# Smaller first loads at the front and a reordered tail in a fused attention and gated-MLP kernel

## The chip, the core and the metric

The kernel runs on one core of a Trainium2 chip. The metric is the device time of one execution in microseconds (us). Engines: PE does matmuls, DVE and ACT do element-wise work, POOL is little used here, SP and ACT issue the DMA transfers. In this kernel PE writes its products into banks of a memory called PSUM (names beginning with ps_), from where DVE and ACT read them. The clock "granted" to PE is the share of full speed that its throttle let through. "PV" is the product of the attention weights and V. A "tile" is 128 rows of x.

## The reference

```python
xn = layernorm(x)                                   # x: 2048 x 512, bf16
s  = softmax((xn @ wq) K^T * 128**-0.5) V @ wo      # 32 heads of 128, 2048 cached keys
g  = silu( (relu(xn @ W_gate) * (xn @ W_up)) @ W_down )   # 512 -> 1792 -> 512
return x + s * g
```

## The kernel before

The program is: a head (layer norm of the first four tiles and the first three 128-column blocks of gate and up), the rest of the gated MLP, 32 heads of attention, and a tail (the output projection of the last heads, times g, plus x). Only head and tail concern us.

Loads of the front, in order of issue. `FCS` cuts the 14 weight blocks into load groups of 3, 5 and 6 blocks; a row of the first group is 3 x 128 x 2 = 768 bytes:

```python
FCS = [0, min(3, FC), min(8, FC), FC]
load_x0(sp, 0);  load_x0(act, 1)                 # one 128-row tile each
load_w(sp, Wg, 0);  load_w(act, Wu, 0)           # gate on SP's queue, up on ACT's
load_x0(sp, 2);  load_x0(act, 3)
load_w(sp, Wg, 1);  load_w(sp, Wu, 1);  load_xq(1)   # ... and the rest, all on SP
```

The head's PE order (`warm_mm` are dummy matmuls that raise the PE clock; `head_transpose` ends in a copy on ACT):

```python
_wait(pe, warm_w);  warm_mm(10)                  # operand cleared by DVE
ctok = {0: head_transpose(0, head_center(0))}
warm_mm(2)
for n in range(4):
    if n + 1 < 4: ntok = head_center(n + 1)      # statistics and centering on DVE
    _wait(pe, ctok[n])
    head_tile(n, 0)                              # gate and up of tile n, block 0
    if n + 1 < 4: ctok[n + 1] = head_transpose(n + 1, ntok)
    for fc in range(1, 3): head_tile(n, fc)
# then blocks 3..13, 512 rows at a time, through a ring of three PSUM bank pairs
```

The tail, for each of the last eight tiles (PE projects, DVE multiplies by g and adds to x, SP stores):

```python
mtok = dve.tensor_tensor(fin_tmp[fb], ps_r[bank], g_sb[n], mult)
_wait(dve, mtok)
ftok = dve.tensor_tensor(x_sb[n], x_sb[n], fin_tmp[fb], add)   # then SP stores x_sb[n]
...
for n in range(NT - 8, NT - 4, 2): emit_M([final n, final n + 1])
flush_last_transposes()              # PE transposes and ACT copies for the last four tiles
for n in range(NT - 4, NT, 2):     emit_M([final n, final n + 1])
```

The softmax here doesn't subtract the row's maximum and nothing guards it: scores larger than these inputs give would overflow.

Of the kernel before, what the change touches and what calls it, by code (L numbers as in the profile page):

```python
# [5 lines left out]
BF16 = mybir.dt.bfloat16  # L6
F32 = mybir.dt.float32
ALU = mybir.AluOpType
ACTF = mybir.ActivationFunctionType
# [42 lines left out]
def bass_recurrent_scan__mha_block_cached__glu_gated_reglu__prompt_kernel(  # L52
# [12 lines left out]
    _, S, D = A_x.shape  # L65
# [39 lines left out]
    with ExitStack() as es:  # L105
        _cnt = [0]

        def S_(shape, dt, name):
            _cnt[0] += 1
            return es.enter_context(nc.sbuf_tensor(f"{name}_{_cnt[0]}", shape, dt))  # L110
# [4 lines left out]
        def newsem(unit=1):  # L115
            _cnt[0] += 1
            return _Sem(es.enter_context(nc.semaphore(f"sem{_cnt[0]}")), unit)
# [13 lines left out]
        Wq_sb = [S_([128, DC, Dh], BF16, "Wq_sb") for _ in range(2)]  # L131
        Wo_sb = [S_([128, G, D], BF16, "Wo_sb") for _ in range(2)]
        PT = [S_([128, 2, NQ], BF16, "PT") for _ in range(NPB)]
        warm = S_([128, D], BF16, "warm")
        es_b = ExitStack()

        def SB_(shape, dt, name):
# [19 lines left out]

        sem_x = [newsem(16) for _ in range(QB)]
        sem_x0 = [newsem(16) for _ in range(4)]
        sem_wg = [newsem(16) for _ in range(3)]  # L160
        sem_wu = [newsem(16) for _ in range(3)]
        sem_xq = [newsem(16) for _ in range(QB)]
        sem_wd = newsem(16)
        sem_kt = [newsem(16), newsem(16)]
# [37 lines left out]
        with nc.Block() as block:  # L202

            @block.tensor
            def _(_pe_eng):
# [10 lines left out]
                for b in range(2):  # L216
                    tok_pool = sem_pool.sig(pool.memset(V_sb[b][:, :, Dh:VW], 2.0))

                FCS = [0, min(3, FC), min(8, FC), FC]
                HFC = 3  # L220
                wg_src = B_W_gate.rearrange("(c p) f -> p c f", p=128)
                wu_src = B_W_up.rearrange("(c p) f -> p c f", p=128)
# [1 line left out]
                def load_w(eng, dst, src, sems, k):  # L224
                    a, b_ = FCS[k] * 128, FCS[k + 1] * 128
                    if b_ > a:
                        sems[k].sig(eng.dma_start(dst[:, :, a:b_], src[:, :, a:b_]))
# [1 line left out]
                x0_tok = {}  # L229
                x_tok = {}  # L230

                def load_x0(eng, n):
                    x0_tok[n] = sem_x0[n].sig(eng.dma_start(x_sb[:, n:n + 1, :], x_t[:, n:n + 1, :]))

                def load_xq(Q):
                    x_tok[Q] = sem_x[Q].sig(
                        sp.dma_start(x_sb[:, 4 * Q:4 * Q + 4, :], x_t[:, 4 * Q:4 * Q + 4, :]))

                warm_w = sem_ln1.sig(dve.memset(warm[:], 0.0))
                load_x0(sp, 0)  # L240
                load_x0(act, 1)
                load_w(sp, Wg_sb, wg_src, sem_wg, 0)
                load_w(act, Wu_sb, wu_src, sem_wu, 0)
                load_x0(sp, 2)
                load_x0(act, 3)
                load_w(sp, Wg_sb, wg_src, sem_wg, 1)
                load_w(sp, Wu_sb, wu_src, sem_wu, 1)
                if QB > 1:
                    load_xq(1)
                load_w(sp, Wg_sb, wg_src, sem_wg, 2)  # L250
                load_w(sp, Wu_sb, wu_src, sem_wu, 2)
                for Q in range(2, QB):
                    load_xq(Q)
                sem_wd.sig(sp.dma_start(Wd_sb[:], B_W_down.rearrange("(c p) d -> p c d", p=128)))
# [101 lines left out]
                def head_transpose(n, ntok):  # L356
# [12 lines left out]
                    acc_free[n % 2] = sem_xa.sig(act.copy(xcT[:, :, n * 128:(n + 1) * 128], src))  # L369
                    return acc_free[n % 2]  # L370

                def warm_mm(k):
                    for _i in range(k):
                        pe.matmul(ps_r[:, 2 * NSLOT - 1, 0:D], warm[:, 0:128], warm[:], start=True, stop=True)

                def head_ln():
                    ctok = {0: head_transpose(0, head_center(0))}
                    warm_mm(2)
                    for n in range(4):
                        if n + 1 < 4:  # L380
                            ntok = head_center(n + 1)
                        _wait(pe, ctok[n])
                        head_tile(n, 0)
                        if n + 1 < 4:
                            ctok[n + 1] = head_transpose(n + 1, ntok)
                        for fc in range(1, HFC):
                            head_tile(n, fc)

                half_slots = []

                def head_tile(n, fc):
                    hs = slice(n * 128, (n + 1) * 128)
                    fs = slice(fc * 128, (fc + 1) * 128)
                    if n == 0:
                        half_slots.append(ring_acquire())
                    s = half_slots[fc]
                    for i, (W, sems) in enumerate(((Wg_sb, sem_wg), (Wu_sb, sem_wu))):
                        if n == 0 and fc == 0:
                            pe.wait_ge(sems[0].h, 16)
                        ins = None  # L400
                        for c in range(DC):
                            ins = pe.matmul(ps_r[:, 2 * s + i, hs], W[:, c, fs], xcT[:, c, hs],  # L402
                                            start=(c == 0), stop=(c == DC - 1))
                        if n == 3:
                            half_tok[(fc, i)] = (sem_gate if i == 0 else sem_gu).sig(ins)
# [39 lines left out]
                sig_free = [None, None]  # L445
                hT_free = [None, None]

                def finish_gate_up(Q, fc, s, gtok, gu_tok):
                    par = Q % 2
                    gb = 2 * s  # L450
                    gk = fc % NSLOT
                    _wait(act, gtok)
                    _wait(act, gr_free[gk])
                    rtok = sem_relu.sig(act.activation(gr_sb[gk][:], ps_r[:, gb, :], ACTF.Relu))  # L454
                    _wait(dve, gu_tok)
                    _wait(dve, rtok)
                    if fc == 0:
                        _wait(dve, hT_free[par])
                    h_tok = sem_h.sig(
                        dve.tensor_tensor(hT[par][:, fc, :], gr_sb[gk][:], ps_r[:, gb + 1, :], ALU.mult)  # L460
                    )
                    gr_free[gk] = h_tok
                    ring_tok[s] = [rtok, h_tok]
                    if Q == 0:
                        ln_task(fc)
                    return h_tok

                def emit_gate_up(Q):
                    qs = slice(Q * NQ, (Q + 1) * NQ)
                    h_tok = None  # L470
                    for fc in range(FC):
                        fs = slice(fc * 128, (fc + 1) * 128)
                        if Q == 0 and fc < HFC:
                            s = half_slots[fc]
                            finish_gate_up(Q, fc, s, half_tok[(fc, 0)], half_tok[(fc, 1)])
                            continue
                        s = ring_acquire()
                        gb = 2 * s
                        if fc == 0:
                            _wait_all(pe, xt_ready[Q])  # L480
                        xT, xs = (xcT, slice(0, NQ)) if Q == 0 else (xnT, qs)
                        if Q == 0 and fc in FCS:
                            k = FCS.index(fc)
                            pe.wait_ge(sem_wg[k].h, 16)
                            pe.wait_ge(sem_wu[k].h, 16)
                        ins = None
                        for c in range(DC):
                            ins = pe.matmul(ps_r[:, gb, :], Wg_sb[:, c, fs], xT[:, c, xs],  # L488
                                            start=(c == 0), stop=(c == DC - 1))
                        gtok = sem_gate.sig(ins)  # L490
                        for c in range(DC):
                            ins = pe.matmul(ps_r[:, gb + 1, :], Wu_sb[:, c, fs], xT[:, c, xs],  # L492
                                            start=(c == 0), stop=(c == DC - 1))
                        gu_tok = sem_gu.sig(ins)
                        h_tok = finish_gate_up(Q, fc, s, gtok, gu_tok)
                    return h_tok
# [39 lines left out]
                    hT_free[par] = ytok  # L536

                assert DC == 4 and QB >= 2 and FC >= 4 * (QB - 1) + 2
                _wait(pe, warm_w)
                warm_mm(10)  # L540
                head_ln()
                for Q in range(QB):
                    hlast = emit_gate_up(Q)
# [5 lines left out]
                rz_sb = S_([128, 4, 1], F32, "rz_sb")  # L549
                Onorm = [S_([128, 4, Dh], BF16, "Onorm") for _ in range(NON)]  # L550
                OT_store = [S_([128, G, S], BF16, "OT_store") for _ in range(2)]
                fin_tmp = [S_([128, D], BF16, "fin_tmp") for _ in range(2)]

                qt_ready = {}
                qp_done_tok = {}
# [213 lines left out]
                def emit_final_tile(n, bank):  # L769
# [8 lines left out]
                    for hh in range(G):  # L778
# [6 lines left out]
                    _wait(dve, fin_free[fb])  # L785
                    mtok = sem_opa.sig(
                        dve.tensor_tensor(fin_tmp[fb][:], ps_r[:, bank, 0:D], g_sb[:, n, :], ALU.mult))  # L787
                    _wait(dve, mtok)
                    if n == 0:
                        _wait(dve, base_done[NT - 1])  # L790
# [3 lines left out]
                    if Q == QB - 1 or j % 2 == 1:  # L794
                        n0 = n if Q == QB - 1 else n - 1
                        _wait(sp, ftok)
                        sem_out.sig(sp.dma_start(out_t[:, n0:n + 1, :], x_sb[:, n0:n + 1, :]))
                    return mtok

                plan = {}  # L800
                for b in range(NBLK):
# [47 lines left out]
                assert not plan  # L849
                for n in range(NT - 8, NT - 4, 2):  # L850
                    emit_M([(emit_final_tile, n), (emit_final_tile, n + 1)])
                flush_last_transposes()
                for n in range(NT - 4, NT, 2):
                    emit_M([(emit_final_tile, n), (emit_final_tile, n + 1)])
                sp.wait_ge(sem_out.h, sem_out.n)


# [26 lines left out]
```

## Time and profile before

| | before |
|---|---|
| median of the first 3 runs | 1287.48 us (1286.75 to 1287.56) |
| span of the profiled execution | 1286.0 us |
| first 512-wide gate matmul | 13.63 us |
| first gate matmul of the second 512 rows | 44.70 us |
| from the start of the last 32 PV matmuls (shown at 1272.37) to the end | 13.58 us |

The page rounds spans to 0.1 us. Stretches up to the end of the span are worked out here with the unrounded spans of the packed traces: 1285.957 us before, 1288.623 us after the change.

The page's busy table and its chain that ended last, of the kernel before:

```profile
PE 1279.3 (99%) x12040; PEld 835.4 (65%) x12040; DVE 382.0 (30%) x685; ACT 1001.7 (78%) x1109; POOL 13.2 (1%) x25
PE 98%; DVE 1%; DMA 0%; issue 0%; ACT 0%; ACTq 0%
```

PE bounds the kernel. What a change at the ends can win is PE's idle time there. The waits of PE, kernel before (engine, tile, line, who was waited for, total us, times, longest us):

```profile
PE ps_r L374 <- DVE warm L239: 1.2, 1, 1.2
PE ps_r L402 <- DMA Wu_sb<-in_B_W_up_dram: 0.5, 1, 0.5
PE ps_r L779 <- ACT OT_store L719: 0.4, 1, 0.4
PE ps_r L488 <- ACT gr_sb L454: 0.4, 1, 0.4
PE ps_r L402 <- ACT xcT L369: 0.2, 1, 0.2
```

Five waits, all at the two ends. The PE timeline of the front, kernel before (start us, length us, engine, line, operation, out<-in, shapes, count, and in brackets the idle time before it and who ended it):

```profile
1.19 4.23 PE L374 MATMUL ps_r<-warm 128*128 128x512 bf16 x10 [1.19 <-DVE warm L239]
5.26 0.39 PE L364 MATMUL ps_acc<-ident,xc_sb 128*128 128x128 bf16 x4
...
6.33 0.40 PE L402 MATMUL ps_r<-xcT,Wg_sb 128*128 128x128 bf16 x4 [0.25 <-ACT xcT L369]
7.23 0.40 PE L402 MATMUL ps_r<-xcT,Wu_sb 128*128 128x128 bf16 x4 [0.51 <-DMA Wu_sb<-in_B_W_up_dram]
...
13.63 1.02 PE L488 MATMUL ps_r<-xcT,Wg_sb 128*128 128x512 bf16 x4 [0.41 <-ACT gr_sb L454]
```

Ten warm-up matmuls take 0.42 us each, which is half rate; later ones of the same size start every 0.22 us. The first tile must wait for the up weights until 7.23, and the first 512-wide matmul waits for a PSUM bank pair until 13.63.

In the tail DVE is the limit. The end of its timeline, kernel before (multiply L787, add L792):

```profile
1281.72 0.68 DVE L787 TENSOR_TENSOR fin_tmp<-ps_r,g_sb 128x512 bf16<-128x512 f32 x1
1282.43 0.43 DVE L792 TENSOR_TENSOR x_sb<-x_sb,fin_tmp 128x512 bf16<-128x512 bf16 x1
1282.78 0.68 DVE L787 TENSOR_TENSOR fin_tmp<-ps_r,g_sb 128x512 bf16<-128x512 f32 x1
1283.49 0.42 DVE L792 TENSOR_TENSOR x_sb<-x_sb,fin_tmp 128x512 bf16<-128x512 bf16 x1
```

Read the differences of the starts: from a multiply to the add that depends on it 0.71, from that add to the next multiply 0.35, so 1.06 us a tile. Compare two independent DVE instructions of the same length, near 13 us of the same kernel, which start 0.60 us apart:

```profile
12.84 0.69 DVE L460 TENSOR_TENSOR hT<-gr_sb,ps_r 128x512 bf16<-128x512 bf16 x1 [3.27 <-PE ps_r L402]
13.44 0.69 DVE L319 BATCH_NORM_STATS2 stats<-x_sb 128x6 f32<-128x512 bf16 x1
```

### The profile page before, as it was taken

Reading aid. Unit: us, or ns where it says so; the run is one execution under the profiler, and the core shown is the slowest. Engines: PE = TensorE matmul, PEld = TensorE weight load, DVE = VectorE, ACT = ScalarE, POOL = GpSimd, SP = SyncE. Lnnn points to the kernel's source line nnn. Section 1 sums busy time; section 2 is a strip of 40 time slices with the busy share of each in tenths; the row PEclk is TensorE's granted clock in tenths of the full one; section 3 lists DMA queues with packets and bytes.
Section 4 is the critical chain, followed back from the end, with each engine's and each line's share of the span. In section 5 each row is a group of like instructions: output and inputs, shape, how many; then the busy total and the mean of one; then the engine's idle time right before and its main releaser. Section 6 shows DMA issues by size and latency. Waiting matters only on the chain.

```text
span 1286.0 us, 26948 instructions
## 1 busy us (share of the span) xinstructions
PE 1279.3 (99%) x12040; PEld 835.4 (65%) x12040; DVE 382.0 (30%) x685; ACT 1001.7 (78%) x1109; POOL 13.2 (1%) x25
## 2 busy tenths in 40 slices
PE   9999999999999999999999999999999999999998
PEld 5444466666666666666666666666666666666665
DVE  6433311112222222222222222222222222234456
ACT  3322399998888888888888888888888888888884
POOL 2100000000000000000000000000000000000000
PEclk9999999999999999999999999999999999999999
DMA  9600123332222332332221322323323212332302
GB/s 262 131 1 1 21 44 52 63 57 38 37 54 47 71 54 50 55 70 51 54 46 33 64 47 53 55 67 55 55 50 71 54 34 38 52 65 55 50 14 74
DMA packets 240977, 72.13 MB, mean 56 GB/s; under 512 B 227808, under 2 KB 240864, under 8 KB 240864
## 3 DMA queue, kind: packets, MB, share of 16 engines
q1 hardware_dynamic: 240048, 69.76, 28.4%
q8 instruction: 96, 1.57, 0.5%
q10 hardware_dynamic: 816, 0.66, 0.2%
q14 instruction: 17, 0.14, 0.0%
HBM read 32.77 MB, written 2.10 MB: 27 GB/s over the span
## 4 chain that ended last, share of the span: by engine, by line
PE 98%; DVE 1%; DMA 0%; issue 0%; ACT 0%; ACTq 0%
PE ps_acc L742 36%; PE ps_r L645 34%; PE ps_r L578 9%; PE ps_r L599 8%; PE ps_acc L511 4%; PE ps_r L488 4%; PE ps_r L492 4%; PE ps_r L779 1%; DMA Wu_sb<-in_B_W_up_dram 0%; DVE fin_tmp L787 0%; PE ps_r L402 0%; ACT gr_sb L454 0%; DVE x_sb L792 0%; PE ps_acc L364 0%; DVE Onorm L696 0%
## 5 line engine op out<-in xcount | busy, mean ns | idle before, releaser
L655 ACT ACTIVATE PT<-ps_r 128x1024 bf16<-128x1024 f32 x1024 | 952.5, 1054 | 167.7 <-PE ps_r L645 167.7
L742 PEld LDWEIGHTS ps_acc<-V_sb,PT 128*128 128x128 bf16 x8192 | 621.1, 98 | 241.7 <-ACT PT L655 3.5
L742 PE MATMUL ps_acc<-V_sb,PT 128*128 128x129 bf16 x8192 | 776.7, 220 | 0.0
L645 PE MATMUL ps_r<-QT_sb,KT_sb 128*128 128x512 bf16 x2048 | 754.2, 379 | 0.0
L672 DVE RECIPROCAL rz_sb<-ps_acc 128x4 f32<-128x4 f32 x127 | 23.3, 184 | 729.5 <-PE ps_acc L742 729.5
L645 PEld LDWEIGHTS ps_r<-QT_sb,KT_sb 128*128 128x128 bf16 x2048 | 194.9, 98 | 1.1 <-DVE QT_sb L589 0.4
L578 PE MATMUL ps_r<-xnT,Wq_sb 128*128 128x512 bf16 x512 | 130.9, 379 | 0.0
L599 PE MATMUL ps_r<-Wo_sb,OT_store 128*128 128x512 bf16 x448 | 114.6, 379 | 0.0
L589 DVE CAST QT_sb<-ps_r 128x512 bf16<-128x512 f32 x128 | 88.5, 692 | 48.1 <-PE ps_r L578 48.1
L578 PEld LDWEIGHTS ps_r<-xnT,Wq_sb 128*128 128x128 bf16 x512 | 49.9, 97 | 60.6 <-ACT PT L655 27.1
L675 DVE TENSOR_TENSOR Onorm<-ps_acc,rz_sb 128x512 bf16<-128x512 f32 x127 | 87.8, 691 | 4.4
L599 PEld LDWEIGHTS ps_r<-Wo_sb,OT_store 128*128 128x128 bf16 x448 | 43.8, 98 | 52.9 <-ACT PT L655 0.2
L454 ACT ACTIVATE gr_sb<-ps_r 128x512 bf16<-128x512 f32 x56 | 32.9, 595 | 49.9 <-PE ps_r L488 49.3
L612 DVE TENSOR_TENSOR s_acc<-s_acc,ps_r 128x512 f32<-128x512 f32 x96 | 66.0, 688 | 17.3 <-PE ps_r L599 17.3
L460 DVE TENSOR_TENSOR hT<-gr_sb,ps_r 128x512 bf16<-128x512 bf16 x56 | 38.4, 686 | 47.2 <-PE ps_r L492 42.1
L511 PE MATMUL ps_acc<-Wd_sb,hT 128*128 128x512 bf16 x224 | 49.0, 379 | 0.0
L492 PE MATMUL ps_r<-xnT,Wu_sb 128*128 128x512 bf16 x168 | 43.1, 379 | 0.0
L488 PE MATMUL ps_r<-xnT,Wg_sb 128*128 128x512 bf16 x168 | 43.1, 379 | 0.0
L511 PEld LDWEIGHTS ps_acc<-Wd_sb,hT 128*128 128x128 bf16 x224 | 21.9, 98 | 26.4
L519 ACT ACTIVATE sig_sb<-ps_acc 128x512 f32<-128x512 f32 x12 | 7.2, 597 | 29.5 <-PE ps_acc L511 29.5
L488 PEld LDWEIGHTS ps_r<-xnT,Wg_sb 128*128 128x128 bf16 x168 | 16.4, 98 | 19.8
L492 PEld LDWEIGHTS ps_r<-xnT,Wu_sb 128*128 128x128 bf16 x168 | 16.4, 98 | 19.8
(50 smaller groups left out, 182.2 us busy)
## 6 DMA issues: line engine op xcount, KB each, us to landing
V_sb<-in_A_v_cache_dram SPq DMA_DIRECT2D x32, 512.0 KB, 4.8
Wq_sb<-in_A_wq_dram SPq DMA_DIRECT2D x32, 128.0 KB, 2.5
Wo_sb<-in_A_wo_dram SPq DMA_DIRECT2D x8, 512.0 KB, 5.0
OT_store<-Onorm SPq DMA_TRANSPOSE x127, 2.4
Wd_sb<-in_B_W_down_dram SPq DMA_DIRECT2D x1, 1792.0 KB, 14.3
x_sb<-in_A_x_dram SPq DMA_DIRECT2D x3, 512.0 KB, 11.4
out_dram<-x_sb SPq DMA_DIRECT2D x6, 256.0 KB, 2.2
Wg_sb<-in_B_W_gate_dram SPq DMA_DIRECT2D x1, 768.0 KB, 10.9
```

Of the source, the lines that this page charges most:

```text
L460: dve.tensor_tensor(hT[par][:, fc, :], gr_sb[gk][:], ps_r[:, gb + 1, :], ALU.mult)
L488: ins = pe.matmul(ps_r[:, gb, :], Wg_sb[:, c, fs], xT[:, c, xs], start=(c == 0), stop=(c == DC - 1))
L492: ins = pe.matmul(ps_r[:, gb + 1, :], Wu_sb[:, c, fs], xT[:, c, xs], start=(c == 0), stop=(c == DC - 1))
L511: ins = pe.matmul(ps_acc[:, jb, 0:D], hT[par][:, fc, j * 128:(j + 1) * 128], Wd_sb[:, fc, :], start=(fc == 0), stop=(fc == FC - 1))
L578: ins = pe.matmul(ps_r[:, bank, :], Wq_sb[b][:, c, :], xnT[:, c, qs], start=(c == 0), stop=(c == DC - 1))
L589: etok = sem_qpe.sig(dve.tensor_copy(QT_sb[b][:, qs], ps_r[:, bank, :]))
L599: ins = pe.matmul(ps_r[:, bank, 0:D], OT_store[g % 2][:, hh, n * 128:(n + 1) * 128], Wo_sb[g % 2][:, hh, :], start=(hh == 0), stop=(hh == ...
L612: dve.tensor_tensor(s_acc[:, n, :], s_acc[:, n, :], ps_r[:, bank, 0:D], ALU.add)
L645: ins = pe.matmul(ps_r[:, 2 * s + tt, :], KT_sb[h % 2][:, t * 128:(t + 1) * 128], QT_sb[h % 2][:, qs], start=True, stop=True)
L655: act.activation(PT[pb][:], ps_r[:, 2 * s:2 * s + 2, :], ACTF.Exp, scale=scale)
L675: dve.tensor_tensor(Onorm[ob][:], o_ap, rz_sb[:].to_broadcast([128, 4, Dh]), ALU.mult))
L742: ins = pe.matmul(o_ap, PT[pb][:, tt, j * 128:(j + 1) * 128], V_sb[vb][:, t, 0:VW], start=(t == 0 and j % 2 == 0), stop=(t == KT - 1 and j ...
```

## The change

The intent is to begin and to end sooner. Front: x tile 0 comes in two halves over both queues; the first weight group has only one block (256-byte rows), then comes a group of two (512-byte rows); warm-up multiplies a constant instead of a cleared buffer; the head tiles are reordered around the later arrival of blocks 1 and 2; block 3 goes to the two idle accumulator banks. Tail: the add of a tile is issued after the multiply of the next one (with four buffers instead of two for the products), and the last transposes stand between the filler pairs, the first two pairs of the last eight tiles, whose projections do not need those transposes. The diff is shortened and in part put as pseudocode:

```diff
-FCS = [0, min(3, FC), min(8, FC), FC]
+FCS = [0, 1, 3, 8, FC]
-load_x0(sp, 0); load_x0(act, 1)
-load_w(sp, Wg, 0); load_w(act, Wu, 0)
-load_x0(sp, 2); load_x0(act, 3)
-load_w(sp, Wg, 1); load_w(sp, Wu, 1); load_xq(1)
+load_x0(sp, 0, 0, 64); load_x0(act, 0, 64, 128); load_x0(sp, 1)
+load_w(act, Wu, 0); load_w(sp, Wg, 0); load_x0(act, 2)
+load_w(sp, Wg, 1); load_w(act, Wu, 1); load_x0(act, 3)
+load_w(sp, Wg, 2); load_w(sp, Wu, 2); load_xq(1)       # ... rest as before
-_wait(pe, warm_w); warm_mm(10)
+warm_mm(9)                                             # constant 1.0
 # head order (Tn = transposes of tile n, n.f = gate and up of tile n, block f)
-T0 warm warm | 0.0 T1 0.1 0.2 | 1.0 T2 1.1 1.2 | 2.0 T3 2.1 2.2 | 3.0 3.1 3.2
+T0 warm | 0.0 T1 0.1 | 1.0 1.1 0.2 T2 1.2 | 2.0 2.1 T3 2.2 | 3.0 3.1 3.2
 # first 512-wide block
-s = ring_acquire()
+if Q == 0 and fc == HFC: use ps_acc banks 0, 1; wait acc_free
 # tail
-_wait(dve, mtok); add(n)
+flush_final_add()            # the add of the tile before
+fin_pending.append(n)        # this one's add comes after the next multiply
 ... final(NT-8), final(NT-7)
+flush_last_transposes()
 ... final(NT-6), final(NT-5)
-flush_last_transposes()
 ... last four finals
+flush_final_add()
```

More of the change, by code (lines that the diff above doesn't have):

```diff
@@ L133, in bass_recurrent_scan__mha_block_cached__glu_gated_reglu__prompt_kernel @@
         PT = [S_([128, 2, NQ], BF16, "PT") for _ in range(NPB)]
-        warm = S_([128, D], BF16, "warm")
         es_b = ExitStack()
@@ L159, in bass_recurrent_scan__mha_block_cached__glu_gated_reglu__prompt_kernel @@
         sem_x0 = [newsem(16) for _ in range(4)]
-        sem_wg = [newsem(16) for _ in range(3)]
-        sem_wu = [newsem(16) for _ in range(3)]
+        sem_wg = [newsem(16) for _ in range(4)]
+        sem_wu = [newsem(16) for _ in range(4)]
         sem_xq = [newsem(16) for _ in range(QB)]
@@ L230, in _, with load_x0 @@
                 x_tok = {}
-                def load_x0(eng, n):
-                    x0_tok[n] = sem_x0[n].sig(eng.dma_start(x_sb[:, n:n + 1, :], x_t[:, n:n + 1, :]))
+                def load_x0(eng, n, lo=0, hi=128):
+                    x0_tok[n] = sem_x0[n].sig(eng.dma_start(x_sb[lo:hi, n, :], x_t[lo:hi, n, :]))
                 def load_xq(Q):
@@ L237, in load_xq @@
                         sp.dma_start(x_sb[:, 4 * Q:4 * Q + 4, :], x_t[:, 4 * Q:4 * Q + 4, :]))
-                warm_w = sem_ln1.sig(dve.memset(warm[:], 0.0))
-                load_x0(sp, 0)
-                load_x0(act, 1)
+                load_x0(sp, 0, 0, 64)
+                load_x0(act, 0, 64, 128)
+                load_x0(sp, 1)
+                load_w(act, Wu_sb, wu_src, sem_wu, 0)
                 load_w(sp, Wg_sb, wg_src, sem_wg, 0)
-                load_w(act, Wu_sb, wu_src, sem_wu, 0)
-                load_x0(sp, 2)
+                load_x0(act, 2)
+                load_w(sp, Wg_sb, wg_src, sem_wg, 1)
+                load_w(act, Wu_sb, wu_src, sem_wu, 1)
                 load_x0(act, 3)
-                load_w(sp, Wg_sb, wg_src, sem_wg, 1)
-                load_w(sp, Wu_sb, wu_src, sem_wu, 1)
-                if QB > 1:
-                    load_xq(1)
                 load_w(sp, Wg_sb, wg_src, sem_wg, 2)
                 load_w(sp, Wu_sb, wu_src, sem_wu, 2)
+                load_xq(1)
+                load_w(sp, Wg_sb, wg_src, sem_wg, 3)
+                load_w(sp, Wu_sb, wu_src, sem_wu, 3)
                 for Q in range(2, QB):
@@ L370, in head_transpose @@
                     return acc_free[n % 2]
+                ones_w = nc.const_aps.tensor(1.0, [128, 128], BF16)
+                ones_r = nc.const_aps.tensor(1.0, [128, NQ], BF16)
                 def warm_mm(k):
                     for _i in range(k):
-                        pe.matmul(ps_r[:, 2 * NSLOT - 1, 0:D], warm[:, 0:128], warm[:], start=True, stop=True)
+                        pe.matmul(ps_r[:, 2 * NSLOT - 1, :], ones_w, ones_r, start=True, stop=True)
                 def head_ln():
-                    ctok = {0: head_transpose(0, head_center(0))}
-                    warm_mm(2)
-                    for n in range(4):
-                        if n + 1 < 4:
-                            ntok = head_center(n + 1)
-                        _wait(pe, ctok[n])
-                        head_tile(n, 0)
-                        if n + 1 < 4:
-                            ctok[n + 1] = head_transpose(n + 1, ntok)
-                        for fc in range(1, HFC):
-                            head_tile(n, fc)
+                    c0 = head_transpose(0, head_center(0))
+                    n1 = head_center(1)
+                    warm_mm(1)
+                    _wait(pe, c0)
+                    head_tile(0, 0)
+                    c1 = head_transpose(1, n1)
+                    n2 = head_center(2)
+                    head_tile(0, 1)
+                    _wait(pe, c1)
+                    head_tile(1, 0)
+                    head_tile(1, 1)
+                    head_tile(0, 2)
+                    c2 = head_transpose(2, n2)
+                    n3 = head_center(3)
+                    head_tile(1, 2)
+                    _wait(pe, c2)
+                    head_tile(2, 0)
+                    head_tile(2, 1)
+                    c3 = head_transpose(3, n3)
+                    head_tile(2, 2)
+                    _wait(pe, c3)
+                    for fc in range(HFC):
+                        head_tile(3, fc)
                 half_slots = []
@@ L397, in head_tile @@
                     for i, (W, sems) in enumerate(((Wg_sb, sem_wg), (Wu_sb, sem_wu))):
-                        if n == 0 and fc == 0:
-                            pe.wait_ge(sems[0].h, 16)
+                        if n == 0 and fc in FCS:
+                            pe.wait_ge(sems[FCS.index(fc)].h, 16)
                         ins = None
@@ L446, in _, with gu_banks @@
                 hT_free = [None, None]
+                def gu_banks(s):
+                    if s is None:
+                        return ps_acc[:, 0, :], ps_acc[:, 1, :]
+                    return ps_r[:, 2 * s, :], ps_r[:, 2 * s + 1, :]
                 def finish_gate_up(Q, fc, s, gtok, gu_tok):
                     par = Q % 2
-                    gb = 2 * s
+                    g_ps, u_ps = gu_banks(s)
                     gk = fc % NSLOT
@@ L453, in finish_gate_up @@
                     _wait(act, gr_free[gk])
-                    rtok = sem_relu.sig(act.activation(gr_sb[gk][:], ps_r[:, gb, :], ACTF.Relu))
+                    rtok = sem_relu.sig(act.activation(gr_sb[gk][:], g_ps, ACTF.Relu))
                     _wait(dve, gu_tok)
@@ L459, in finish_gate_up @@
                     h_tok = sem_h.sig(
-                        dve.tensor_tensor(hT[par][:, fc, :], gr_sb[gk][:], ps_r[:, gb + 1, :], ALU.mult)
+                        dve.tensor_tensor(hT[par][:, fc, :], gr_sb[gk][:], u_ps, ALU.mult)
                     )
                     gr_free[gk] = h_tok
-                    ring_tok[s] = [rtok, h_tok]
+                    if s is None:
+                        y_bank_free[:] = [h_tok, h_tok]
+                    else:
+                        ring_tok[s] = [rtok, h_tok]
                     if Q == 0:
@@ L476, in emit_gate_up @@
                             continue
-                        s = ring_acquire()
-                        gb = 2 * s
+                        if Q == 0 and fc == HFC:
+                            s = None
+                            _wait_all(pe, acc_free)
+                        else:
+                            s = ring_acquire()
+                        g_ps, u_ps = gu_banks(s)
                         if fc == 0:
@@ L487, in emit_gate_up @@
                         for c in range(DC):
-                            ins = pe.matmul(ps_r[:, gb, :], Wg_sb[:, c, fs], xT[:, c, xs],
+                            ins = pe.matmul(g_ps, Wg_sb[:, c, fs], xT[:, c, xs],
                                             start=(c == 0), stop=(c == DC - 1))
@@ L491, in emit_gate_up @@
                         for c in range(DC):
-                            ins = pe.matmul(ps_r[:, gb + 1, :], Wu_sb[:, c, fs], xT[:, c, xs],
+                            ins = pe.matmul(u_ps, Wu_sb[:, c, fs], xT[:, c, xs],
                                             start=(c == 0), stop=(c == DC - 1))
@@ L538, in _ @@
                 assert DC == 4 and QB >= 2 and FC >= 4 * (QB - 1) + 2
-                _wait(pe, warm_w)
-                warm_mm(10)
+                warm_mm(9)
                 head_ln()
@@ L551, in _ @@
                 OT_store = [S_([128, G, S], BF16, "OT_store") for _ in range(2)]
-                fin_tmp = [S_([128, D], BF16, "fin_tmp") for _ in range(2)]
+                fin_tmp = [S_([128, D], BF16, "fin_tmp") for _ in range(4)]
                 qt_ready = {}
@@ L787, in emit_final_tile, with flush_final_add @@
                         dve.tensor_tensor(fin_tmp[fb][:], ps_r[:, bank, 0:D], g_sb[:, n, :], ALU.mult))
+                    flush_final_add()
+                    fin_pending.append((n, fb, mtok))
+                    return mtok
+                fin_pending = []
+                def flush_final_add():
+                    if not fin_pending:
+                        return
+                    n, fb, mtok = fin_pending.pop()
+                    Q, j = divmod(n, 4)
                     _wait(dve, mtok)
@@ L797, in emit_final_tile @@
                         sem_out.sig(sp.dma_start(out_t[:, n0:n + 1, :], x_sb[:, n0:n + 1, :]))
-                    return mtok
                 plan = {}
@@ L851, in _ @@
                     emit_M([(emit_final_tile, n), (emit_final_tile, n + 1)])
-                flush_last_transposes()
+                    if n == NT - 8:
+                        flush_last_transposes()
                 for n in range(NT - 4, NT, 2):
                     emit_M([(emit_final_tile, n), (emit_final_tile, n + 1)])
+                flush_final_add()
                 sp.wait_ge(sem_out.h, sem_out.n)
```

## The prediction

> **What bounds the kernel now.** The busy table gives PE 1279.3 of 1286.0 us (99%), ACT 78%, DVE 30%; the chain that ended last is 98% PE. PE's own waits add up to under 3 us, all in the first 14 or last 8 us. The change touches only these two ends. The roughly 1260 us between them are the same instructions and should merely begin earlier.
>
> **Front, from the timeline.** Warm-up matmuls run from 1.19 us (held for a DVE memset), 0.43 us each. x tile 0 lands at 3.3, is centered by 4.6, transposed at 5.26, copied by ACT until 6.26. The first gate tile starts at 6.33; then PE waits 0.51 us for the up weights (three blocks, 384 KB), until 7.23. PE is then full until about 13.2 and waits 0.41 us for a ring slot (ACT relu of block 0), so the first 512-wide gate matmul starts at 13.63.
>
> After: warm-up starts at about 0.8 and is one matmul shorter. One-block weights (128 KB each) should land by 4.5, so the first tile starts at about 5.7 with its weights there. New is a wait for blocks 1-2: the queues must move 1152 KB first. Summing the before trace's GB/s (37, 247, 254, 364, 350: 1.25 MB by 6 us) gives 6.0 to 6.6 us. Then the remaining head work (11 tiles at 0.44, two transposes at 0.22), with two or three waits of 0.2-0.3 us for ACT copies, because one tile now covers some 0.58 us copies. Block 3 goes to idle accumulator banks, which removes the 0.41 us wait. First 512-wide gate matmul at about 12.5: gain 1.1 us (0.5 to 1.5). Nothing downstream waits, so it is kept whole.
>
> **End.** DVE is the limit: after the last normalisations, eight final tiles run at a period of 1.06 us (multiply to dependent add 0.72, add to next multiply 0.34), from 1275.35 to 1283.92; the last store ends the span 2.1 us later. Where two DVE instructions of this size are independent (relu product, then statistics, near 13 us) the start-to-start gap is 0.60. Adding one tile late makes nearly every pair independent: 0.12 us x 8, 0.95 us at most. The Trainium skill's "VectorE: DVE Perf Modes", section "The DRAIN you can't avoid", measured no cost of a semaphore after each of eight copies; the trace here has 0.72 against 0.60, and I follow the trace. Earlier transposes remove PE's 0.44 us wait for the ACT copy, needed so that PE (0.86 us a tile) feeds the faster DVE (0.94); tile 10 still comes about 0.2 us late. The last two stores now issue almost together (0.37 us an issue): 0.1-0.3 us lost. Net 0.5 us (0.2 to 0.9).
>
> **Sum.** 1.1 + 0.5 = 1.6 us, all on the chain: 1287.5 - 1.6 = 1285.9 us, range 1284.8 to 1287.0. Faster by over 2%: 0.005; within 2%: 0.99; slower: 0.005.
>
> **What would show it.** First 512-wide gate matmul near 12.5, no wait on relu; first head tile near 5.7; a PE wait on Wg/Wu just after it. End: multiply-to-next gap 0.60; the last add about 0.7 us closer to the last PV matmul; PE's wait on the OT copy gone. Middle: same length.
>
> **What would make it wrong.** Matmuls are at half rate until about 5.4 us. "TensorE: Matmul & The Clock Gate", Part 1, calls the clock's window free-running; if shorter warm-up and the new gap leave PE at half rate for the first tiles, up to 2 us is lost. Or 256-byte weight rows transfer slowly and blocks 1-2 land after 7 us. Or the stores at the end collide.

## The result

| | before | after |
|---|---|---|
| median | 1287.5 us (1286.75 to 1287.57, 6 runs) | 1290.15 us (1288.7 to 1291.77, 6 runs) |
| span of the profiled execution | 1286.0 | 1288.6 |
| first 512-wide gate matmul | 13.63 | 16.85 |
| from there to the first gate matmul of the second 512 rows | 31.07 | 31.08 |
| start of the last 32 PV matmuls to the end | 13.58 | 13.03 |

The change is slower: the ratio is 1.002, and its 95% interval, 1.0007 to 1.0033, excludes 1. Ratios here are the mean time of one kernel's runs over that of the other's of the same rounds, so not quite the ratio of the medians quoted. The table accounts for the profiled executions: the front lost 3.22 us, the middle is the same, the tail won 0.55; together 2.67, which is the difference of the unrounded spans (1285.957 us before, 1288.623 us after the change). The six runs fall in two kinds: two with a mean clock of 1.000 at 1288.7 and 1288.9, four with 0.997 to 0.999 at 1290.1 to 1291.8. The one profiled is of the second kind; that the clock fell in the three others is read from mean clock and time together, not from traces (the kernel before also has a run with a mean of 0.999, at 1287.24). Even the two runs at 1.000 are slower than every run of the kernel before. The waits of PE, kernel after:

```profile
PE ps_r L417 <- DMA Wg_sb<-in_B_W_gate_dram: 2.8, 1, 2.8
PE ps_r L377 <- PEq L907: 0.8, 1, 0.8
PE ps_r L417 <- ACT xcT L369: 0.7, 2, 0.5
PE ps_acc L364 <- DVE xc_sb L354: 0.4, 1, 0.4
```

The waits for the memset, the relu and the OT copy are gone, as intended; one wait of 2.8 us for weights is new. The front on PE, kernel after:

```profile
0.78 3.52 PE L377 MATMUL ps_r<-const-bfloat16-1.0 128*128 128x512 bf16 x9 [0.78 <-PEq L907]
4.74 0.38 PE L364 MATMUL ps_acc<-ident,xc_sb 128*128 128x128 bf16 x4 [0.44 <-DVE xc_sb L354]
...
5.80 0.40 PE L417 MATMUL ps_r<-xcT,Wg_sb 128*128 128x128 bf16 x4 [0.46 <-ACT xcT L369]
6.03 0.39 PE L417 MATMUL ps_r<-xcT,Wu_sb 128*128 128x128 bf16 x4
...
9.44 0.40 PE L417 MATMUL ps_r<-xcT,Wg_sb 128*128 128x128 bf16 x4 [2.80 <-DMA Wg_sb<-in_B_W_gate_dram]
...
11.04 0.63 PE L417 MATMUL ps_r<-xcT,Wg_sb 128*128 128x128 bf16 x4
11.47 0.63 PE L417 MATMUL ps_r<-xcT,Wu_sb 128*128 128x128 bf16 x4
...
16.85 1.03 PE L515 MATMUL ps_acc<-xcT,Wg_sb 128*128 128x512 bf16 x4
```

The first tile does start earlier (5.80 instead of 6.33) and finds its up weights. Then blocks 1 and 2 come only at 9.4. And near 11 us a group of four matmuls takes 0.43 us from start to start instead of the 0.22 before: the clock has fallen. The stretches view of the kernel after, cut at the clock's changes (stretch, length, busy us of PE, PEld, DVE, ACT, POOL with counts, then granted clock, DMA share and GB/s):

```profile
3.68:7.10 3.41, 2.06 (x20) 1.06 (x18) 3.10 (x9) 2.37 (x4) 0.00 (x0) 1.00 0.94 252
7.10:10.51 3.41, 1.06 (x19) 1.07 (x20) 1.32 (x4) 0.17 (x1) 0.00 (x0) 1.00 1.05 364
10.51:13.92 3.41, 3.41 (x36) 3.33 (x33) 0.01 (x1) 0.58 (x1) 0.00 (x0) 0.50 1.08 361
```

In the second stretch PE worked 1.06 of 3.41 us; in the third the clock is 0.50 although PE never rests. At half rate for 3.41 us, about 1.7 us of work is lost.

The tail, end of the DVE timeline of the kernel after:

```profile
1284.17 0.68 DVE L813 TENSOR_TENSOR fin_tmp<-ps_r,g_sb 128x512 bf16<-128x512 f32 x1
1284.77 0.41 DVE L829 TENSOR_TENSOR x_sb<-x_sb,fin_tmp 128x512 bf16<-128x512 bf16 x1
1285.10 0.68 DVE L813 TENSOR_TENSOR fin_tmp<-ps_r,g_sb 128x512 bf16<-128x512 f32 x1
1285.70 0.75 DVE L829 TENSOR_TENSOR x_sb<-x_sb,fin_tmp 128x512 bf16<-128x512 bf16 x2
```

Now 0.60 and 0.33, so 0.93 us a tile: the dependence is gone. The last two adds stand together.

Where are the weights? The DMA issues of the front, first of the kernel before, then of the kernel after (size, and us from issue to landing):

```profile
Wu_sb<-in_B_W_up_dram ACTq DMA_DIRECT2D x1, 384.0 KB, 6.0
Wg_sb<-in_B_W_gate_dram SPq DMA_DIRECT2D x1, 384.0 KB, 4.8
```

```profile
Wu_sb<-in_B_W_up_dram ACTq DMA_DIRECT2D x1, 256.0 KB, 6.1
Wg_sb<-in_B_W_gate_dram SPq DMA_DIRECT2D x1, 256.0 KB, 6.7
Wu_sb<-in_B_W_up_dram ACTq DMA_DIRECT2D x1, 128.0 KB, 3.0
Wg_sb<-in_B_W_gate_dram SPq DMA_DIRECT2D x1, 128.0 KB, 3.3
```

Before, SP issued the whole 384 KB at 1.18 us. After, it issued the 256 KB of blocks 1 and 2 at 2.72, and these fewer bytes took longer, 6.7 us instead of 4.8.

### The profile page after: what moved, and what is told of

Read it like the earlier page. It is cut to its first block, busy times and chain, and to the rows that moved or that the text cites. A ratio compares the mean times of both kernels' runs of the same rounds, so it can differ in the third digit from the quotient of the medians. Undisturbed runs are those within 1.5% of the kernel's fastest.

```text
span 1288.6 us, 26943 instructions
## 1 busy us (share of the span) xinstructions
PE 1280.0 (99%) x12038; PEld 836.2 (65%) x12038; DVE 380.2 (30%) x684; ACT 1001.6 (78%) x1109; POOL 13.2 (1%) x25
## 4 chain that ended last, share of the span: by engine, by line
PE 98%; DVE 1%; DMA 1%; SPq 0%; issue 0%; ACT 0%; DVEq 0%
PE ps_acc L768 36%; PE ps_r L671 34%; PE ps_r L604 9%; PE ps_r L625 8%; PE ps_acc L538 4%; PE ps_r L519 3%; PE ps_r L515 3%; PE ps_r L805 1%; DMA Wg_sb<-in_B_W_gate_dram 1%; PE ps_r L417 0%; DVE fin_tmp L813 0%; DVE x_sb L829 0%; SPq L232 0%; PE ps_acc L519 0%; PE ps_acc L515 0%
```

## The experiments

Theory: the front's loss is the late landing of blocks 1 and 2, because their rows are short and long-row loads are in flight beside them, and the clock falls because PE is idle too much meanwhile. Rivals: the new head order or warm-up costs the time; the order of issue and the split of x delay the loads; short rows are slow by themselves; the tail costs something. Eleven kernels ran, each in five rounds beside the kernel before. They ran in three sets on different chips, in which the medians of the kernel before were 1287.23, 1287.25 and 1287.51, so comparisons between sets are good to about 0.3 us. Each kernel has one traced execution.

### 1. The old loads in the changed kernel

```diff
 # the changed kernel, loads and FCS as before
-FCS = [0, 1, 3, 8, FC]    +FCS = [0, 3, 8, FC]
-split x tile 0, one-block first group ...
+load_x0(sp, 0); load_x0(act, 1); load_w(sp, Wg, 0); load_w(act, Wu, 0); ...
```

> The changed kernel with the input loads of the kernel before (whole x tile 0 on SP, tile 1 on ACT, first weight group of three blocks, old order); head schedule, accumulator banks, warm-up and tail stay changed. Theory (late weights are the cause): PE waits for weights until about 7.2 us instead of 9.4, no fall of the clock, first 512-wide gate matmul at 12.7 to 13.2, time 1286.0 to 1286.6, spread under 1 us. Rival (new head schedule, shorter warm-up or accumulator banks cost the time): stays at 1288.5 or more.

Measured: median 1287.06 us (before 1287.25), four runs at 1286.9 to 1287.2 and one, the profiled one, at 1289.18. Undoing the loads takes away 3.1 of the 1290.15 us, so the loads are the cause, not head order, banks or warm-up alone. Two parts of the expectation failed. The time is 0.5 us above what I expected. PE had the gate weights at 7.08, about as expected; the trace shows two waits of 0.23 us for the ACT copy in the new head order, which would account for it, but the traced run is the disturbed one, so this is not shown for the other four. And the clock did fall in the profiled run, after a wait of only 1.32 us, which put the first 512-wide gate matmul at 15.60 and the spread at 2.3 us. The tail of the change alone gave 1286.96 in the same rounds (experiment 7): with the old loads, the rest of the new front wins nothing. The stretch before the fall in the traced run and the one after:

```profile
4.47:7.89 3.41, 1.62 (x21) 1.13 (x21) 2.21 (x6) 0.59 (x1) 0.00 (x0) 1.00 1.07 361
7.89:11.30 3.41, 3.41 (x35) 3.22 (x33) 1.80 (x6) 0.58 (x1) 0.00 (x0) 0.50 1.08 358
```

### 2. The wait filled with dummy matmuls

```diff
 c1 = head_transpose(1, n1)
 n2 = head_center(2)
+warm_mm(13)
 head_tile(0, 1)
```

> The changed kernel with 13 dummy matmuls (0.22 us each) put into PE's wait for weight blocks 1 and 2. Theory (the idle wait lets the clock fall to half in most executions, for 3.4 us): weights still land near 9.4, clock 1.00 in every execution, first 512-wide gate matmul near 15.2 instead of 16.85, time 1288.7 to 1289.0 with a spread under 0.5 us. Rival (the spread and the half rate come from something else than idleness): spread stays 1288.7 to 1291.8, or the clock still falls.

Measured: 1289.45 us, five runs within 0.44 us (1289.10 to 1289.54; the changed kernel spread over 3.07), clock 1.000 in all five. The two kinds of execution are gone, so idleness of PE made them; the weights are as late as ever (the last, the up weights, were issued at 2.79 and took 7.0 us). The time missed the expected range by 0.45 us: the clock rose only at 5.35 us in the profiled run, which made the first tile start at 6.17, the fillers ended at 9.69, and the first 512-wide gate matmul came at 15.86 instead of 15.2.

### 3. Wide rows in the order of the change

```diff
-FCS = [0, 1, 3, 8, FC]    +FCS = [0, 3, 8, FC]     # split of x and queue order kept
-load_w(sp, Wg, 1); load_w(act, Wu, 1)              # the two-block group is gone
```

> The changed kernel with a first weight group of three blocks (768-byte rows) at the place where the one-block group was, and no second group; x tile 0 still split over two queues, tile 1 still on SP. Theory (short rows of 256 and 512 bytes move slowly and are many): all three blocks land at 6.8 to 7.5, PE waits for them once, time 1286.3 to 1286.9. Rival (order of issue and the split of x, not row size, delay them): they land after 8.5, time 1288 or more.

Measured: the three blocks land so that PE starts at 7.69, a little after the expected 6.8 to 7.5, against 9.44 for blocks 1 and 2 with short rows and the same bytes ahead of them in SP's queue. Cutting the group is worth 1.75 us here. Not all of that is the rows: the cut also needs one issue more on each queue. The gate weights went out at 2.00 here and those of blocks 1 and 2 at 2.72 in the change; from issue to landing they took 5.6 and 6.7 us. Against experiment 1 (7.08) the order and the split cost 0.6. The time, 1289.84 us, was nevertheless nowhere near the expected 1286.3 to 1286.9: all work now waits, PE was busy only 0.95 of the 3.41 us before the clock fell, and the profiled run has half rate from 7.6 to 11.0 us. All five runs show a mean clock of 0.999.

### 4. Short rows in the kernel before

```diff
 # the kernel before
-FCS = [0, 3, 8, FC]       +FCS = [0, 1, 3, 8, FC]
 load_w(sp, Wg, 0); load_w(act, Wu, 0)              # now one block
+load_w(sp, Wg, 1); load_w(act, Wu, 1)              # the other two, same place
```

> The kernel before with only one thing changed in its loads: the first weight group of three blocks is issued as a group of one (256-byte rows) and a group of two (512-byte rows), in the same place, on the same queues, x whole; PE waits for blocks 1 and 2 before its second tile. Theory (short rows delay the bytes): blocks 1 and 2 land after 8.2 us, PE waits 1 us or more for them, first 512-wide gate matmul after 14.5, time 1288.3 to 1290. Rival (the split of x and the order of issue delay them): they land by 7.5 us and the time is 1287.5 or less.

Measured: 1288.64 us (1287.78 to 1289.0), before 1287.23. PE got the gate weights of block 1 at 8.19 and the up weights at 8.72, waiting 1.40 us; the first 512-wide gate matmul came at 14.87. Same queues, same order, whole x: cutting the group alone delays the bytes (gate weights 6.5 us from issue to landing for 256 KB, before 4.8 for 384 KB) and makes the kernel before slower, as expected; the ranges do not overlap (before 1286.81 to 1287.55), though the ratio, 1.0009, has a 95% interval of 0.9995 to 1.0022.

### 5. The split of x undone in the changed kernel

```diff
-load_x0(sp, 0, 0, 64); load_x0(act, 0, 64, 128); load_x0(sp, 1)
+load_x0(sp, 0); load_x0(act, 1)
```

> The changed kernel with x tile 0 loaded whole on SP and tile 1 on ACT, as before; nothing else. Theory (short rows are the larger part, the split of x costs about 1 us of issue on SP): the issue of the weights of blocks 1 and 2 moves from 2.7 to about 1.7 us, they land at 8.3 to 9.0 instead of 9.44, time 1288.2 to 1289.8. Rival (the split and order are the whole cause): they land by 7.3 and the time is 1287.3 or less. If tile 0 itself was helped by the split, the first statistics start later than 3.3 us.

Measured: 1292.03 us, worse than the change itself. The expected time range, 1288.2 to 1289.8, was a miss, and it is the instructive one. The issue moved as expected and PE had the gate weights at 8.37, but the up weights only at 10.01. SP, no longer held up, began to issue the 1280-byte rows of blocks 3 to 7 at 2.20 us, before ACT issued its up weights of blocks 1 and 2 at 2.29. The DMA view of this kernel from 7 to 8 us, with q1 SP's queue and q10 ACT's:

```profile
q1 hardware_dynamic: 206, 0.24, 68.8%
q10 hardware_dynamic: 211, 0.11, 37.2%
```

The two queues moved the same number of packets (206 and 211), but SP's were mostly of 1280 bytes and ACT's of 512, so SP got more than twice the bytes (0.24 against 0.11 MB). The Trainium skill's "DMA: Bandwidth & Descriptors", section "Queues, rings and completion order", states that each DMA engine round-robins between the queue rows at packet granularity; these counts fit that. They cannot show the turns themselves: a packet in the profile is here one row of 512 or 1280 bytes, and the page speaks of packets of several descriptors. The split itself brought tile 0 nothing: statistics started at 3.29 us after the change, 3.30 before, 3.42 here.

### 6. Long rows held back

```diff
 # the changed kernel
 load_x0(act, 3)
+sp.wait_ge(sem_wu[1], 16); sp.wait_ge(sem_wg[1], 16)
 load_w(sp, Wg, 2)                                   # 1280-byte rows
```

> The changed kernel with SP made to wait until weight blocks 1 and 2 (short rows, both queues) have landed before it issues the 1280-byte-row loads of blocks 3 to 7 and all that follow. Theory (short rows of one queue lose to long rows of the other, packet for packet): blocks 1 and 2 land at 6.8 to 7.8 us instead of 9.44, PE waits 1 us or less for them, clock stays at 1.00 in most executions, time 1287 to 1288.3 although the later weights now start late. Rival (512-byte rows are slow by themselves): they land after 8.5 us, time 1289 or more.

The waits of PE in this run:

```profile
PE ps_r L517 <- DVE hT L482: 1.0, 1, 1.0
...
PE ps_r L419 <- DMA Wg_sb<-in_B_W_gate_dram: 0.2, 1, 0.2
```

Measured: PE got the gate weights of block 1 at 7.02 and the up weights at 7.51, with 0.2 us of counted wait, and the clock was 1.000. So the same short rows, alone, land about 2 us earlier: what delays them is mostly the loads that SP issues behind them. The rival, that they are slow by themselves, falls as the main cause. That it is the length of those rows, and not just more bytes in flight, this run does not show; only the counts of experiment 5 speak for it. The time, 1288.92 us, missed its range upwards all the same. SP issued the following loads at 7.5 us instead of 3.3, so the second 512 rows of x came late: on DVE their statistics waited for the load until 15.24, the next products stood behind them, and PE waited 1.0 us for a product near 21 us. Two of the five runs took 1289.80 and 1289.87, also at a clock of 1.000, so not every spread is the clock's; what made those two is open. The hold is a probe, not a remedy.

### 7. The tail alone, and its halves

The kernel before with the tail of the change:

> The kernel before with only the tail of the change (adds one tile late, four buffers, transposes between the filler pairs). Theory: the tail is a gain of 0.5 to 0.7 us, so 1286.8 to 1287.0; multiply starts every 0.94 us instead of 1.06. Rival (the tail costs, by colliding stores or by a later add within the attention part): 1287.5 or more.

Only the late adds:

> The kernel before with only the adds one tile late, last transposes where they were. Theory (the adds are the gain, but PE then arrives late with tiles 12 and 13 because it waits for the transposes' copy): last PV matmul to last add shorter by 0.3 to 0.6 us, one visible DVE wait at tile 12, time 1286.8 to 1287.2. Rival (transposes carry the gain): within 0.1 us of before.

Only the earlier transposes:

> The kernel before with only the last transposes moved between the filler pairs. Theory: DVE is the limit of the tail at 1.06 us a tile, so PE's earlier end buys nothing: last PV matmul to last add within 0.1 us of before, time 1287.2 to 1287.6. Rival: 0.3 us or more faster.

```diff
 # both: the tail part of the change, on the kernel before
 # adds only: flush_last_transposes() stays behind the second filler pair
 # transposes only: the add stays directly behind its own multiply
```

| | start of the last 32 PV matmuls to the end, us | median, us | before in the same rounds |
|---|---|---|---|
| before | 13.58 | | |
| adds only | 13.52 | 1287.45 | 1287.23 |
| transposes only | 13.58 | 1287.43 | 1287.23 |
| both | 13.04 | 1286.96 | 1287.25 |

The unrounded spans are 1285.957, 1285.621, 1285.444 and 1284.636 us. Both together win 0.54 us; the halves win 0.07 and 0.01. With the adds alone DVE outruns PE, which still waits 0.44 us for the transposes' copy; the DVE timeline of that run at tile 12:

```profile
1278.48 0.41 DVE L803 TENSOR_TENSOR x_sb<-x_sb,fin_tmp 128x512 bf16<-128x512 bf16 x1
1279.26 0.69 DVE L787 TENSOR_TENSOR fin_tmp<-ps_r,g_sb 128x512 bf16<-128x512 f32 x1 [0.37 <-PE ps_r L779]
```

With the transposes alone PE ends earlier and DVE keeps its 1.06 us a tile. The expected times held for "both" and "transposes only". "Adds only" missed its range by 0.25 us, and its last add came 0.23 us closer to the PV matmuls where I expected 0.3 to 0.6. The timed medians cannot rank such small things: before's own front varies, since the up weights landed in time for a start at 7.23 in one profiled run and at 6.46 in that of "both", with the same loads.

### 8. The carried add taken out of the tail

With the late adds, tile 7's add is carried into the DVE-bound tail. This run does it in the attention part:

```diff
 if items:
     emit_M(items)
+    if not plan: flush_final_add()
```

> The kernel before with the tail of the change, and the add of tile 7 done in the attention part right after the last pair there, not carried into the tail. Theory (the carried add costs one 0.33 us slot of the tail's DVE chain): last PV matmul to last add 0.3 us shorter than with the tail alone, time 1286.4 to 1286.8. Rival (DVE then waits for PE at some tile, so nothing is won): 1286.9 or more.

Measured: 1286.47 us, inside the range, which would have seemed to confirm the theory. The trace says otherwise: from the start of the last 32 PV matmuls to the last add's end it is 10.85 us, the same as with the tail alone. DVE merely waits elsewhere:

```profile
1274.60 1.45 DVE L787 TENSOR_TENSOR fin_tmp<-ps_r,g_sb 128x512 bf16<-128x512 f32 x2
1275.96 0.41 DVE L803 TENSOR_TENSOR x_sb<-x_sb,fin_tmp 128x512 bf16<-128x512 bf16 x1
1276.44 0.69 DVE L787 TENSOR_TENSOR fin_tmp<-ps_r,g_sb 128x512 bf16<-128x512 f32 x1
```

Two multiplies take 1.45 us instead of the 1.28 of two back to back (0.60 and 0.68), and the next comes 0.48 after the add instead of 0.33: tiles 9 and 10 are not ready on PE. The rival was right about the trace. What the run won beyond the tail lies in its front, whose code is that of the kernel before: the first 512-wide gate matmul came at about 12.87 (one record is missing) against 13.63. The time held by luck.

### 9. A version meant to be better than both

```diff
 # the changed kernel, old loads (as in 1), early flush (as in 8), and this head:
+T0 warm warm | gate 0.0 0.1 0.2, T1, up 0.0 0.1 0.2 | 1.0 T2 1.1 1.2 | 2.0 T3 2.1 2.2 | 3.0 3.1 3.2
```

> Meant as a version better than both: loads as before (768-byte rows, x whole); order of the head tiles as before, but for tile 0 the three gate blocks first, then the transposes of tile 1, then the three up blocks; warm-up from the constant, two filler matmuls; block 3 to the accumulator banks; tail of the change with the early add. Theory: PE has work while the second weight tensor lands, the clock stays at 1.00, first 512-wide gate matmul at 12.0 to 12.7, time 1285.2 to 1286.2. Rival (the load that lands last varies by up to 1 us and eats it): 1286.5 or more.

Measured: 1286.06 us (1285.95 to 1286.32), against 1287.51 (1286.80 to 1287.88) for the kernel before in the same rounds: the two ranges do not overlap. The ratio is 0.9991, with a 95% interval of 0.9978 to 1.0003, which includes 1. The first 512-wide gate matmul starts about 12.74 us (31.08 before the start of the second 512 rows at 43.82; one matmul record is missing at its own start), a little later than expected; PE had the gate weights at 6.53. The old head had its first 512-wide gate matmul at 12.85 in the trace of "both" and at 13.63 in that of the kernel before, so the new front is little better than the old one at its best. That it varies less would explain the narrow range, but is not shown. The stretch before the first gate matmuls shows how near the clock was to falling, and it did not:

```profile
3.58:6.99 3.41, 1.95 (x18) 0.94 (x17) 2.10 (x6) 0.79 (x2) 0.00 (x0) 1.00 1.06 357
```

### What the clock answers to

In every profiled run the clock changed only at multiples of 3.41 us after it first rose. PE's busy time in the last full-rate stretch before each fall in the front, and in the emptiest stretches without a fall after them:

| run | PE busy of 3.41 us | clock after |
|---|---|---|
| wide rows (3) | 0.95 (28%) | fell |
| after, second stretch | 1.06 (31%) | fell |
| whole x (5) | 1.46 (43%) | fell |
| old loads (1) | 1.62 (47%) | fell |
| filler (2), 1281.93 to 1285.34 | 1.78 (52%) | kept |
| combined (9) | 1.95 (57%) | kept |
| after, first stretch | 2.06 (60%) | kept |
| short rows (4), second stretch | 2.14 (63%) | kept |

In these traces the line lies between 47% and 52% busy. (At the very end of each kernel, when PE has finished, the clock falls too, after stretches with PE busy 30% or less.) In experiment 5 a half-rate stretch with 2.37 us busy (69%) was followed by another half-rate one; the full ones (3.35 to 3.41) were followed by full rate. The phase of the stretches differs from run to run (the clock first rose between 3.58 and 6.16 us over the profiled runs). So the same wait can fill most of one stretch in one run and be shared by two in another, which would make the changed kernel's two kinds of run. This is inferred: only one execution of that kernel was traced.

## Why the prediction was wrong, point by point

- **The failed step: "the queues must move 1152 KB first ... gives 6.0 to 6.6 us."** The weights of blocks 1 and 2 landed at 9.4. The sum took the byte rate of 768-byte rows for rows of 256 and 512 bytes, and counted only bytes ahead in the two queues, as if loads issued later took nothing from them. Experiments 3 and 4 show that cutting the group is worth 1.75 us in the order of the change, and makes PE wait 1.4 us when it alone is put into the kernel before; experiment 6 shows that without the loads issued behind them the same rows come at 7.02 and 7.51. The prediction had named this risk ("256-byte weight rows transfer slowly and blocks 1-2 land after 7 us") but put nothing for it into the sum; the late rows were those of 512 bytes, and they are not slow alone. Sharing by packets between queues fits the up weights of experiment 5. It does not by itself explain the change, where the gate weights were last, in the same queue as the long rows and ahead of them.
- **The clock was named as a risk, "up to 2 us", and not put into the sum.** By mean clock and time it fell in four of six runs, and it cost about 1.7 us in the profiled one. It was feared for the first tiles, from the shorter warm-up and the gap; what happened is a fall after them. The wait of 2.8 us caused it; experiment 2 removes the falls with fillers and nothing else. The clock is the smaller part: the two runs at 1.000, 1288.70 and 1288.88, are already above the predicted range.
- **Together**: first 512-wide matmul at 16.85 instead of 12.5, an error of 4.35: 3.1 from the landing (9.4 against the middle 6.3), 1.7 from the clock, less about 0.4 that is left over; after the first tile one wait of 0.23 us for an ACT copy followed, where I had counted two or three.
- **Right in the front**: first tile at 5.8 with its weights there (predicted 5.7), the 0.41 us wait for a ring slot gone, a weight wait just after the first tile, and the middle unchanged, so that a shift in the front is kept whole. It was kept whole as a loss.
- **The tail was right in size and in most of its parts**: predicted 0.5 us (0.2 to 0.9), measured 0.55; last add closer by 0.7, measured 0.69. The start-to-start gap of independent instructions was 0.60 as read before. But no stall showed at tile 10; instead the add of tile 7 was carried into the tail and used up that time, and experiment 8 shows that these two exclude each other. The end lies 2.17 us after the last add in the change, against 2.04 before: the meeting stores cost 0.13, within the predicted 0.1 to 0.3. That the earlier transposes were needed for the gain was right: neither half does it alone.

What stays open: some short-row packets started 2 us after the first long-row ones of the same queue, so the 16 DMA engines probably finished at different times. Which engine moved which packet is not in these traces, so why some lag is not settled. Nor is it settled which of the two weights is last: in the trace of the change it was the gate weights (issued at 2.72, 6.7 us), in that of experiment 2, with the same loads, the up weights. How experiment 9's gain divides among its parts was not measured either.

## What to carry to other kernels

Cutting a first load smaller did not bring the rest sooner here: count issues and rows as well as bytes, and look at which loads will be in flight beside the short rows, those issued later too. A wait early in a kernel has a second price if the PE clock depends on recent work, so cover it with other work or with dummy matmuls, and do not let a run of one or two executions decide. When two engines limit a tail in turn, speed up both in one change, and check the trace and not only the time, because the front's variation of 0.8 us was larger than each of the tail's effects.

## What the Trainium skill lacked or had wrong

- "TensorE: Matmul & The Clock Gate", Part 1, gives the cold state "after ≥1 idle window (~3.4µs)". Its window length and that it is free-running agree with the traces (3.41 us, first rise between 3.58 and 6.16 us). But the window need not be idle: the clock fell after windows with PE busy 28% to 47%, the longest single wait in one of them being 1.32 us, and held at 52% and above. That frequent short idles can do it the page does say elsewhere, but it gives no busy share.
- "DMA: Bandwidth & Descriptors", "Queues, rings and completion order", has the round robin by packets, which fits (206 against 211 packets of the profile, each a row), but not what follows for two queues of unlike rows: 0.24 against 0.11 MB in the same microsecond. "Issuing engines are not separate DMA queues" on that page says that issuing on several engines only saves the sequencer's time; in that microsecond the queue also decided the share.
- "VectorE: DVE Perf Modes", "The DRAIN you can't avoid", measured that a semaphore after each operation costs nothing extra. In the tail here a multiply and its dependent add start 0.71 us apart, a multiply and an independent add 0.60. These are other operations than the page's copies, and the section itself says that an operation that is not held starts earlier, but gives no time for it; the 0.11 us a pair is what was missing.
